# Three buffers instead of two for a unit's sum of values in attention (gated mix of attention and a routed expert layer, one core)

## The chip, the cores and the metric

The kernel runs on one core of one Trainium2 chip. The metric is the time of one execution on the device in microseconds (us). The kernel before takes 1399.78 us, the median of three runs from 1396.5 to 1401.64.

## The reference, cut to what matters

The input x has 2048 rows of 448 numbers. Two branches read it, and a gate per row mixes them.

```python
def _A_ref(x, wqkv, wo):                 # 16 heads of 28
    q, k, v = ...                        # x @ wqkv, by heads
    scores = jnp.einsum("bhqd,bhkd->bhqk", q, k) * scale
    p = _softmax(scores, axis=-1)
    o = jnp.einsum("bhqk,bhkd->bhqd", p, v)
    return o.transpose(0, 2, 1, 3).reshape(B, S, D) @ wo

def _B_ref(x, w_gate, w1, w2):           # 8 experts, the best 2 of each row
    ...
    for e in range(E):
        out = out + w * (_silu(xf @ w1[e]) @ w2[e])

g = _sigmoid((x * gate_w).sum(-1, keepdims=True))
return g * a + (1 - g) * b
```

The change lies in `p @ v`, the sum of the values weighted by the softmax.

## The kernel before, in words

The work has four stages, one after the other on one core: the projections of x to q, k, v and the routing; the experts (with the maxima of the scores computed beside them); attention; and the projection with wo, which also adds the experts' part and writes the output.

**Attention.** The 16 heads are taken in four groups g of four heads, and the 2048 queries in four stretches qc of 512. A *unit* u = 4 g + qc is one group and one stretch, so there are 16 units. A unit has eight steps p, each with two tiles of 128 keys, so there are 128 steps m = 8 u + p. The loop at L1228 emits for each m: `scores(m + 1)`, `beside(m)`, `values(m)`.

- `scores(m)` (L1161) computes the scores of two key tiles for four heads (TensorE, L733) into PSUM, and takes their exponentials on ACT (L1173, L1174, L1176, L1177) into the tile P. One of the eight banks is first copied to SBUF by DVE (X, L1175). At p = 0 it also loads the next unit's queries (`load_q`, L719 and L721, on SP).
- `values(m)` (L1180) multiplies P with the values V (TensorE, L1188) into a bank of PSUM, `po`. DVE then moves that bank into the unit's sum in SBUF, the tile `osb`: a copy at p = 0 (L1192), an addition at the other steps (L1194).
- `beside(m)` (L1196) emits the rest between the two. For the unit before, u - 1, it brings the softmax's denominators, which are a row of `osb`, through DRAM and back: `collect_sums` at p = 0 (POOL issues, L1110 and L1112), `invert_sums` at p = 3 (L1116), `spread_sums` at p = 4 (L1122). At p = 7 `divide(u - 1)` multiplies `osb` by the reciprocals on DVE (L1127), in place, and SP issues four to six transfers (L1137) from it to its rows of the tile OT, which the last stage reads. It also gathers the experts' rows with POOL (`fetch_routed` at p = 1, L1064, tile yg), adds them on DVE at p = 2, 4, 5 and 6 (`routed`, from L1073), and loads the next group's keys and values on SP (`load_k` L704 and L707 at p = 3 and 6, `load_v` L691 at p = 4, and at p = 0 of the next group's first unit).

**The order of the work.** PE, DVE, ACT and POOL execute in the order in which the code emits (`manual_schedule`, L1141); the order of what SP issues is left to the scheduler. A tile name has as many buffers as `bufs` says, by default that of its pool: two in the pool `pc_sb` (L1042), from which `osb`, X and P come. The next use of a buffer waits for the last reader of its former tile. The banks of PSUM that the scores of one key tile and the values share, z0 and z1 (`single`, L1150), have one buffer each and alternate from step to step.

So the tile `osb` of unit u stands in the same buffer as that of unit u - 2. Unit u - 2 is divided, and its transfers to OT are issued, at the last step of unit u - 1. The copy L1192 of unit u comes one step later.

Of the kernel before, what the change touches and what calls it, by code (L numbers as in the profile page):

```python
# [8 lines left out]
F32 = mybir.dt.float32  # L9
# [53 lines left out]
def tile_gated_mha_moe(ctx: ExitStack, tc: tile.TileContext, x, xe_, xT, wv, wqk, wo, w1, w2, out):  # L63
# [213 lines left out]
    with ExitStack() as pa:  # L277
        sb = pa.enter_context(tc.tile_pool(name="pa_sb", bufs=1))
# [459 lines left out]
    with ExitStack() as pb:  # L738
        sb1 = pb.enter_context(tc.tile_pool(name="pb_sb1", bufs=2, reuse_waits="tile"))
        sb = pb.enter_context(tc.tile_pool(name="pb_sb", bufs=2, reuse_waits="tile"))  # L740
# [301 lines left out]
    sb = ctx.enter_context(tc.tile_pool(name="pc_sb", bufs=2, reuse_waits="tile"))  # L1042
# [102 lines left out]
    accs, rc, rs = {}, {}, {}  # L1145
# [4 lines left out]
    def single(i):  # L1150
        return ps.tile([128, 512], F32, name=f"z{i % 2}")
# [28 lines left out]
    def values(m):  # L1180
        u, p = divmod(m, NPR)
        P = Pc.pop(m)
        po = single(m + 1)
        for i in range(2):
            kt = 2 * p + i
            v = held[u // 4][1][kt // 8]
            for j in range(4):
                nc.tensor.matmul(po[32 * j:32 * j + 32], v[:, kt % 8, 32 * j:32 * j + 32], P[4 * i + j],  # L1188
                                 start=i == 0, stop=i == 1)
        if p == 0:  # L1190
            accs[u] = sb.tile([128, 512], F32, name="osb")
            nc.vector.tensor_copy(accs[u], po)  # L1192
        else:
            nc.vector.tensor_tensor(accs[u], po, accs[u], op=ALU.add)  # L1194
# [33 lines left out]
    for m in range(NU * NPR):  # L1228
        if m + 1 < NU * NPR:
            scores(m + 1)  # L1230
        beside(m)
        values(m)
# [70 lines left out]
```

## Time and profile before

| | us |
|---|---|
| median of three runs | 1399.78 |
| the profiled execution | 1399.52 |
| its span, first to last instruction | 1397.7 |
| before attention's steps | 0 to 836 |
| attention's steps | 836 to 1358 |
| the last projection | 1358 to 1397.7 |

The mean granted clock of TensorE over the span is 0.988. The profile is read as follows. PE is TensorE's matrix products, PEld its weight loads, DVE the vector engine, ACT the scalar engine, POOL GpSimd, SP the engine that issues most transfers (SPq: its queue). A row of the order of time gives the start, the duration, the engine, the line, the operation, the tiles written and read, and in brackets how long the engine stood idle before it and what ended that. A row of waits gives who waited for whom, the sum, the times and the longest. A row of stretches gives the bounds, the length, the busy time of PE, PEld, DVE, ACT and POOL with the number of instructions, the granted clock of TensorE (1.00 is full speed), the busy share of the transfer engines and GB/s.

### The profile page before, as it was taken

What the parts mean: (1) busy time and instruction counts of PE and PEld (TensorE: products, weight loads), DVE (VectorE), ACT (ScalarE), POOL (GpSimd) and SP (SyncE); (2) the same over time, 40 slices, a digit from 0 to 9 for tenths busy, and PEclk for the clock granted to TensorE, in tenths of its full rate; (3) what the DMA queues carried; (4) which work ended last, traced back from release to release, by engine and by line L of the source; (5) the groups of instructions that cost most, each with busy time, mean ns of one, the idle gap of its engine ahead of it and who ended that gap; (6) DMA issues with size and microseconds to landing.
All of it is one profiled execution on the core that took longest, in us unless ns stands there. A gap on an engine that the chain in (4) does not pass through costs nothing. (4 is left out here: it accounts for less than half of the span.)

```text
span 1397.7 us, 27189 instructions
## 1 busy us (share of the span) xinstructions
PE 1353.4 (97%) x10166; PEld 892.3 (64%) x10166; DVE 927.0 (66%) x1076; ACT 849.0 (61%) x1270; POOL 616.1 (44%) x661
## 2 busy tenths in 40 slices
PE   9999999999999999999999999997999799979999
PEld 8888788788877777777777774433343333433348
DVE  5737898888988988889887854443444344434445
ACT  5335355345433543434444349997999799969871
POOL 2124676577566876668767531221222222212220
PEclk9999999999999999999999999999999999989999
DMA  9887865653444544445453221233223322422113
GB/s 348 298 282 232 299 181 174 214 176 113 146 139 149 142 150 146 151 155 168 134 165 105 73 81 56 69 86 109 68 66 97 98 57 68 125 68 61 47 50 127
DMA packets 136278, 191.30 MB, mean 137 GB/s; under 512 B 23284, under 2 KB 102680, under 8 KB 135632
## 3 DMA queue, kind: packets, MB, share of 16 engines
q1 hardware_dynamic: 124992, 160.55, 36.3%
q0 software_dynamic: 11008, 28.76, 6.8%
q8 instruction: 80, 1.31, 0.4%
q14 instruction: 54, 0.44, 0.1%
q10 hardware_dynamic: 144, 0.23, 0.1%
HBM read 139.20 MB, written 60.74 MB: 143 GB/s over the span
## 5 line engine op out<-in xcount | busy, mean ns | idle before, releaser
L143 DVE TENSOR_REDUCE mp<-pm 128x3 f32<-128x1536 f32 (+1 forms) x301 | 508.7, 1732 | 11.0 <-PE pm L122 11.0
L1188 PE MATMUL z<-P,V 128*32 128x512 f32 x2032 | 252.4, 615 | 0.2
L733 PE MATMUL z<-Q,Kh 29*128 29x512 f32 x508 | 188.0, 449 | 37.3 <-DVE osb L1192 37.3
L1176 ACT ACTIVATE P<-s 128x1536 f32<-128x1536 f32 x127 | 194.3, 1530 | 27.0 <-PE s L733 26.9
L1174 ACT ACTIVATE P<-s 128x1536 f32<-128x1536 f32 x127 | 193.8, 1526 | 0.0
L733 PE MATMUL s<-Q,Kh 29*128 29x512 f32 x1524 | 191.0, 446 | 0.0
L1175 DVE COPY X<-z 128x512 f32<-128x512 f32 x127 | 87.8, 691 | 153.8 <-PE z L733 142.2
L804 POOL TENSOR_TENSOR w2l<-w2r,w2h 128x448 fp32r<-128x448 f32 x112 | 129.3, 1155 | 118.8 <-ACT w2h L798 92.1
L1020 ACT ACTIVATE yo<-acc 128x448 f32<-128x448 f32 x64 | 34.8, 544 | 232.9 <-PE acc L1006 223.9
L733 PEld LDWEIGHTS z<-Q,Kh 29*128 29x128 f32 x508 | 75.5, 185 | 152.3 <-DVE osb L1192 41.7
L1006 PE MATMUL acc<-w2h,hh 128*128 128x448 f32 x448 | 167.6, 374 | 0.3 <-PEq L818 0.3
L1006 PE MATMUL acc<-w2h,hl 128*128 128x448 f32 x448 | 166.5, 372 | 0.0
L1006 PE MATMUL acc<-w2l,hh 128*128 128x448 f32 x448 | 166.1, 371 | 0.0
L949 ACT ACTIVATE hf<-acc 128x512 f32<-128x512 f32 (+6 forms) x154 | 74.2, 482 | 138.0 <-PE acc L945 130.4
L136 DVE TENSOR_REDUCE mp<-acc 128x1 f32<-128x512 f32 x130 | 89.4, 688 | 85.1 <-PE pm L122 83.6
L813 POOL TENSOR_TENSOR hl<-hf,hh 128x512 fp32r<-128x512 f32 x112 | 144.8, 1293 | 1.0 <-ACT hh L952 1.0
L1188 PEld LDWEIGHTS z<-P,V 128*32 128x32 f32 x2032 | 54.1, 111 | 133.1 <-issue 85.1
L1194 DVE TENSOR_TENSOR osb<-z,osb 128x512 f32<-128x512 f32 x112 | 77.4, 691 | 91.3 <-PE z L1188 91.3
L945 PE MATMUL acc<-xeh,w1h 128*128 128x512 f32 (+3 forms) x408 | 136.8, 339 | 0.0
L945 PE MATMUL acc<-xeh,w1l 128*128 128x512 f32 (+3 forms) x408 | 136.1, 338 | 0.0
L1110 POOL DMA_DIRECT2D sum_d<-osb x64 | 31.0, 491 | 204.5 <-DVE osb L1194 204.3
L772 POOL TENSOR_TENSOR w1l<-w1r,w1h 128x1024 fp32r<-128x1024 f32 (+1 forms) x49 | 90.9, 1854 | 61.5 <-ACT w1h L766 48.0
(221 smaller groups left out, 2777.2 us busy)
## 6 DMA issues: line engine op xcount, KB each, us to landing
w2r<-in_w_dram SPq DMA_DIRECT2D x112, 224.0 KB
w1r<-in_w_dram SPq DMA_DIRECT2D x56, 384.0 KB
ys_d<-zero_d SPq DMA_DIRECT2D x32, 448.0 KB
ys_d<-yo SPq DMA_DIRECT2D x64, 224.0 KB
x_d<-xf SPq DMA_DIRECT2D x115, 64.0 KB
qkh_d<-hi SPq DMA_DIRECT2D x28, 256.0 KB
qkl_d<-lo SPq DMA_DIRECT2D x28, 256.0 KB
w1r<-in_w_dram SPq DMA_DIRECT2D x112, 64.0 KB
```

Of the source, the lines that this page charges most:

```text
L136: nc.vector.tensor_reduce(mp[:, o:o + 1], banks[0], axis=AX.X, op=ALU.max)
L143: nc.vector.tensor_reduce(mp[:, (o + lo) % 256:(o + lo) % 256 + hi - lo], pm[h][:, lo - 3 * h:hi - 3 * h], axis=AX.X, op=ALU.max)
L733: nc.tensor.matmul(banks[j], k[rw, ks], q[rw, c], start=i == 0, stop=i == 2)
L772: nc.gpsimd.tensor_tensor(l[:, :, half], r[:, :, half], h[:, :, half].bitcast(F32), op=ALU.subtract)
L804: nc.gpsimd.tensor_tensor(w2l, w2r, w2h.bitcast(F32), op=ALU.subtract)
L813: nc.gpsimd.tensor_tensor(hl, hf32, hh[:, 0:512].bitcast(F32), op=ALU.subtract)
L945: nc.tensor.matmul(pu[:, 0:HC], a, b[:, cs], start=i == 0, stop=i == len(mms) - 1)
L1006: nc.tensor.matmul(py[:n, 0:D], a[:, cs], b, start=i == 0, stop=i == 3 * NH - 1)
L1174: nc.scalar.activation(P[:, 1:4], t[0], AF.Exp, scale=SCALE)
L1175: nc.vector.tensor_copy(X, z[1])
L1176: nc.scalar.activation(P[:, 4:7], t[1], AF.Exp, scale=SCALE)
L1188: nc.tensor.matmul(po[32 * j:32 * j + 32], v[:, kt % 8, 32 * j:32 * j + 32], P[4 * i + j], start=i == 0, stop=i == 1)
```

## The change

The tile `osb` gets three buffers instead of the pool's two. Nothing else differs.

```diff
         if p == 0:
-            accs[u] = sb.tile([128, 512], F32, name="osb")
+            accs[u] = sb.tile([128, 512], F32, name="osb", bufs=3)
             nc.vector.tensor_copy(accs[u], po)
         else:
             nc.vector.tensor_tensor(accs[u], po, accs[u], op=ALU.add)
```

The tile of unit u then stands in the buffer of unit u - 3. One buffer takes 2 KB in each of the 128 partitions of SBUF.

## The prediction

> **What bounds the kernel now.** I read the page first, for which engine looks full.
>
> ```profile
> span 1397.7 us, 27189 instructions
> ## 1 busy us (share of the span) xinstructions
> PE 1353.4 (97%) x10166; PEld 892.3 (64%) x10166; DVE 927.0 (66%) x1076; ACT 849.0 (61%) x1270; POOL 616.1 (44%) x661
> ```
>
> PE's 97% leaves 44 us, but the share is an average over stages. The change touches only attention's second part (L1161 to L1194), which runs from 836 to 1358 us, so the next view is busy time by stretch: all of attention, then unit 1 alone (eight steps without a stall), units 2 to 14, and two short stretches.
>
> ```profile
> 836.00:1358.00 522.00, 484.49 (x5085) 196.67 (x5078) 226.52 (x366) 471.32 (x509) 108.21 (x182) 0.97 0.27 76
> 865.90:895.38 29.48, 29.48 (x327) 11.97 (x320) 13.83 (x22) 29.48 (x34) 7.19 (x13) 1.00 0.21 61
> 895.38:1326.50 431.12, 396.57 (x4168) 161.67 (x4160) 184.69 (x297) 385.71 (x418) 92.01 (x157) 0.96 0.28 79
> 1063.48:1066.90 3.42, 3.42 (x24) 1.39 (x20) 0.73 (x2) 1.04 (x2) 0.96 (x1) 0.50 0.78 228
> 1333.14:1336.55 3.41, 3.41 (x21) 1.01 (x21) 1.97 (x4) 1.97 (x2) 0.00 (x0) 0.50 0.63 233
> ```
>
> The columns after the length are busy time of PE, PEld, DVE, ACT and POOL, then the granted clock. In unit 1 ACT is busy for all of 29.48 us: the exponentials of one step follow each other without a gap, 29.48 / 8 = 3.685 us a step. PE fills that time too, at full clock. In units 2 to 14 ACT is idle for 431.12 - 385.71 = 45.4 us and the mean clock is 0.96. So the stage has a floor, ACT's 3.685 us a step, and something lifts it off that floor once a unit. The waits name it:
>
> ```profile
> engine line waited for: us in total, times, longest us
> ACT P L1176 <- PE s L733: 26.9, 7, 8.0
> ACT P L1173 <- PE s L733: 23.3, 15, 3.0
> ...
> PE z L733 <- DVE osb L1192: 37.3, 14, 8.5
> ...
> DVE osb L1192 <- DMA OT<-osb: 55.0, 14, 10.1
> ```
>
> ACT waits for PE's scores, PE waits for DVE's copy L1192 to free a bank of z, and the copy waits, in 14 of 16 units, for a transfer. The order of time at the start of unit 7 shows why:
>
> ```profile
> 1054.21 0.68 DVE L1127 TENSOR_TENSOR osb<-osb,rs 128x512 f32<-128x512 f32 x1
> 1054.92 4.11 SPq L1137 DMA_DIRECT2D OT<-osb  x5
> 1061.02 0.69 DVE L1192 COPY osb<-z 128x512 f32<-128x512 f32 x1 [2.09 <-DMA OT<-osb]
> 1061.77 0.49 PE L733 MATMUL z<-Q,Kh 29*128 29x512 f32 x1 [1.42 <-DVE osb L1192]
> ```
>
> The sum of unit 5 is divided in the last step of unit 6, then SP issues five transfers out of it (4.11 us). Unit 7's first copy wants the same buffer one step later, and on DVE it blocks what is queued behind it: the next step's X copy and the additions.
>
> **The change part by part.** With three buffers unit u's first copy writes the buffer of unit u-3, whose transfers went out a whole unit (29 us) earlier. The wait of 55.0 us goes; no instruction, transfer or wait is added, nothing is moved. The price of the wait is not PE's 37.3 us but what the units last beyond 29.48 us. For units 2 to 14: 431.12 - 13 x 29.48 = 47.9 us. For unit 15 the ACT rows give the stalled stretch, two steps long:
>
> ```profile
> 1326.50 1.56 ACT L1174 ACTIVATE P<-s 128x1536 f32<-128x1536 f32 x1
> ...
> 1338.80 1.45 ACT L1174 ACTIVATE P<-s 128x1536 f32<-128x1536 f32 x1
> ```
>
> 12.30 - 2 x 3.685 = 4.9 us. Together 52.8 us: 37.3 of them PE standing still, the rest mostly PE running at half clock after the longer stalls. The two stretches at clock 0.50 above lie behind the stalls of units 7 and 15, whose waits of PE are (in the windows 1050 to 1065 and 1325 to 1340 us):
>
> ```profile
> PE z L733 <- DVE osb L1192: 1.4, 1, 1.4
> ...
> PE z L733 <- DVE osb L1192: 2.9, 1, 2.9
> ```
>
> In unit 1, with no such wait, the clock is 1.00, so I let the half-clock stretches go with the stalls.
>
> [...]
>
> What is late next? First yg: step p=2 of a unit starts adding what POOL gathered shortly before.
>
> ```profile
> 873.66 0.69 DVE L1175 COPY X<-z 128x512 f32<-128x512 f32 x1 [1.12 <-PE z L733]
> 874.27 0.61 DVE L1073 TENSOR_TENSOR yg<-yg 128x448 f32<-128x448 f32 x1
> 875.54 0.69 DVE L1194 TENSOR_TENSOR osb<-z,osb 128x512 f32<-128x512 f32 x1 [0.65 <-PE z L1188]
> ...
> 899.50 1.03 POOL L1064 DMA_INDIRECT yg<-ys_d,slot_i  x1 [0.30 <-issue]
> ...
> 930.73 1.03 POOL L1064 DMA_INDIRECT yg<-ys_d,slot_i  x1 [0.30 <-issue]
> ...
> DMA to landing us min/median/max: 4.0/4.2/5.2
> ...
> 925.45 1.56 ACT L1174 ACTIVATE P<-s 128x1536 f32<-128x1536 f32 x1
> ```
>
> L1073 is due 874.27 - 865.90 = 8.37 us into a stall-free unit, and DVE has 0.65 us to spare before the addition that PE waits for. Unit 2 (from 895.38): due at 903.75, landed at 899.50 + 4.2 = 903.70, on time. Unit 3 (from 925.45): due at 933.82, landed at 934.93; 1.11 - 0.65 = 0.46 us late. Until now the stall hid this. Bounds over 14 units: 0 if all are like unit 2; (930.73 + 5.2 - 933.82 - 0.65) x 14 = 1.46 x 14 = 20.4 us if all issue as late as unit 3 and land at the slowest. I take half the units like unit 2 and half like unit 3: 7 x 0.46 = 3.2, and about half of it, 1.5 us, since the X copy and PE's queue have a little slack of their own.
>
> Second, V's other half at units 4, 8 and 12, issued behind the OT transfers and first needed at p=4.
>
> ```profile
> 1220.57 1.56 ACT L1174 ACTIVATE P<-s 128x1536 f32<-128x1536 f32 x1
> ...
> 880.91 1.92 PE L1188 MATMUL z<-P,V 128*32 128x512 f32 x16
> ...
> 1227.16 0.48 SPq L691 DMA_DIRECT2D V<-v_d  x1
> ...
> 1231.00:1233.60 2.60, 1.11 (x9) 0.83 (x9) 0.69 (x1) 0.00 (x0) 0.00 (x0) 0.50 0.56 164
> 1233.60:1235.60 2.00, 2.00 (x13) 0.40 (x12) 0.69 (x1) 1.83 (x2) 0.00 (x0) 0.50 0.00 0
> ```
>
> In unit 1 p=4 begins 880.91 - 865.90 = 15.0 us in, so in unit 12 without the stall at 1235.6. The DMA share (last column but one) falls to 0.00 after 1233.6: V is there with 2.0 us to spare. I cost it at 0, and 0 to 3 us a boundary as bounds.
>
> Third, memory: a third 2 KB a partition shifts tiles behind osb in the pool, and so which old tile each waits for when attention opens.
>
> ```profile
> 836.04 0.60 ACT L1173 ACTIVATE P<-z 128x512 f32<-128x512 f32 x1 [0.39 <-PE s L733]
> ...
> 838.46 0.96 POOL L1064 DMA_INDIRECT yg<-ys_d,slot_i  x1 [21.50 <-DMA wo_r<-in_wo_dram]
> ```
>
> The last transfers of the stage before have landed when the first gather starts, so a shifted tile costs at most 838.46 - 836.04 = 2.4 us, once. It could also end one of the waits there, so the other bound is the 0.39 us before that first exponential, as a gain. I take 0, since P and X are asked for ahead of osb.
>
> The sum: the profiled execution took 1399.5 us (1.8 us outside its span; the runs' median is 1399.8). 1399.5 - 52.8 + 1.5 = 1348.2. The projections after 1358 us only start earlier.
>
> **The rivals.**
>
> One, the gather becomes the new bound in every unit: for it, unit 3's lateness; against, unit 2's. 1346.7 + 20.4 = 1367. Chance 0.06.
>
> Two, the group boundaries: SP's order is not written out by hand, and the scheduler may plan it anew when a wait goes; V or K then lands after its need. At 2 us of slack, a 5 us slip costs 3 us and, as in unit 7, a half-clock stretch of 3.42 x 0.5 = 1.7 us: 3 x 4.7 = 14, so 1362. For it, DMA is dense there (share 0.56); against, V's issue does not wait for the stalled copy. Chance 0.07.
>
> Three, the half-clock stretches after short waits come from elsewhere and stay: 2 x 1.7 = 3.4 us, 1351.6. Against it, the clock of unit 1. Chance 0.04. [...]
>
> Four, slower than before: PE, no longer resting once a unit, loses clock throughout. PE fills its step of 3.685 us at clock 1.00; over the 112 steps of units 2 to 15 the 52.8 us are used up when a step takes 3.685 + 0.47 = 4.16 us, at a clock below 0.89. At 0.85 a step takes 4.34 us and the time is 1348.2 + 112 x 0.65 = 1421. Against it, 29.48 us without a pause were granted 1.00. Chance 0.02.
>
> Five, the buffer does nothing, because the copy's wait is kept for a reason other than the buffer (the transfers' tile OT, say): 1399.5. Against it, the copy touches only z and osb. Chance 0.03.
>
> **How the numbers follow.** The main case has 0.78, at 1348.2. Its range is 1343.5 (no late gather, and 3 us of spread as the runs show, 1396.5 to 1401.6 around 1399.8) to about 1356 (one unit's slip or a shifted tile on top). Reaching to rival two gives 1343 to 1362; left out are rivals one, four and five and the odd tail. A measurement of this kernel can tell about 0.5%, 7 us, from no change. Faster by more takes the main case and rivals one to three: 0.95. Within 0.5% is rival five and a little more: 0.03. Slower: 0.02.
>
> **What would show it.** Right: no wait of L1192 for OT; in the ACT rows every unit from 1 to 15 lasts 29.5 to 30.2 us; the clock in attention is 1.00; L1073 gets a short wait for yg; attention ends near 1307 us. Wrong: units 4, 8 and 12 still last several us longer (rival two), or all do (rival one), with PE waiting for an L1194 that stands behind L1073; PE at a clock below 1 without an idle stretch ahead of it.

## The result, and the profile after

The changed kernel takes 1353.13 us (median of four runs, 1352.16 to 1354.23); beside it the kernel before took 1400.51 us. The ratio is 0.967, 95% interval 0.965 to 0.969. The profiled execution took 1352.68 us, with a span of 1350.9 us: 46.8 us less than before, where the forecast had 51.3.

The same views as before the change. Busy time by stretch: attention, unit 1, units 2 to 13, unit 14, and one short stretch in unit 14.

```profile
836.00:1310.00 474.00, 471.25 (x5079) 191.41 (x5074) 227.16 (x365) 468.93 (x509) 108.58 (x182) 1.00 0.30 84
865.78:895.27 29.49, 29.49 (x328) 11.92 (x320) 13.88 (x22) 29.49 (x34) 7.19 (x13) 1.00 0.21 61
895.27:1250.96 355.69, 354.81 (x3848) 144.64 (x3840) 170.24 (x272) 354.35 (x385) 84.91 (x145) 1.00 0.33 92
1250.96:1284.27 33.31, 31.46 (x328) 12.44 (x320) 15.11 (x25) 29.71 (x34) 7.08 (x13) 0.95 0.18 50
1260.93:1264.35 3.42, 3.42 (x16) 0.53 (x16) 1.22 (x2) 1.79 (x2) 0.00 (x0) 0.50 0.00 0
```

Attention is 48 us shorter, and ACT's busy time in it is about the same (468.93 us against 471.32): the same work without the gaps. Units 2 to 13 are 355.69 - 12 x 29.48 = 1.9 us above the floor. Unit 14 alone is 3.8 us above it, and has the only stretch of attention at half clock.

The waits of DVE in attention:

```profile
DVE osb L1194 <- PE z L1188: 80.9, 103, 2.3
DVE osb L1192 <- PE z L1188: 11.5, 13, 1.3
...
DVE yg L1073 <- DMA yg<-ys_d,slot_i: 6.5, 7, 2.0
DVE oh L1086 <- DMA OT<-osb: 2.1, 1, 2.1
DVE osb L1192 <- DMA OT<-osb: 1.2, 1, 1.2
```

The copy L1192 no longer waits 55.0 us for OT. What it waits now is the 1.2 us for the product that unit 1 had before as well; the last row is one more wait of that length, and its releaser was only the last to report. Two waits stand where none stood: L1073 for the gathered yg, and L1086 for OT. The second, in the order of time (DVE and SP, in unit 14):

```profile
1249.48 6.14 SPq L1137 DMA_DIRECT2D OT<-osb  x8
...
1255.06 0.69 DVE L1175 COPY X<-z 128x512 f32<-128x512 f32 x1 [1.13 <-PE z L733]
1257.86 0.43 DVE L1086 CAST oh<-OT 128x512 fp32r<-128x512 f32 x1 [2.12 <-DMA OT<-osb]
1258.32 0.56 DVE L180 TENSOR_TENSOR ol<-OT,oh 128x384 fp32r<-128x384 f32 x1
1258.89 0.29 DVE L181 TENSOR_TENSOR oh<-OT,oh 64x128 fp32r<-64x128 f32 x1
1259.21 0.69 DVE L1194 TENSOR_TENSOR osb<-z,osb 128x512 f32<-128x512 f32 x1
```

Unit 12 is divided at the last step of unit 13. It has eight transfers, as each unit of the last group has, and not the four to six that the description gives; they take SP 6.14 us to issue, and the first split of OT for the last projection (`split_o`, at p = 1 of unit 14) needs them. DVE waits 2.12 us, then does 1.3 us of splitting (each value into a rounded part and a rest), and only then the addition that frees PE's bank.

### The profile page after: what moved, and what is told of

The parts are those of the page before. It is cut to its first block, busy times and chain, and to the rows that moved or that the text cites. A ratio compares the mean times of both kernels' runs of the same rounds, so it can differ in the third digit from the quotient of the medians.

```text
span 1350.9 us, 27181 instructions
## 1 busy us (share of the span) xinstructions
PE 1341.4 (99%) x10166; PEld 887.2 (66%) x10166; DVE 928.1 (69%) x1076; ACT 847.5 (63%) x1270; POOL 616.6 (46%) x661
## 5 line engine op out<-in xcount | busy, mean ns | idle before, releaser
L1188 PE MATMUL z<-P,V 128*32 128x512 f32 x2032 | 246.4, 602 | 0.0
L1176 ACT ACTIVATE P<-s 128x1536 f32<-128x1536 f32 x127 | 198.1, 1560 | 0.9 <-PE s L733 0.9
L1174 ACT ACTIVATE P<-s 128x1536 f32<-128x1536 f32 x127 | 196.5, 1547 | 0.0
L733 PEld LDWEIGHTS z<-Q,Kh 29*128 29x128 f32 x508 | 74.5, 183 | 111.9 <-issue 30.2
L1194 DVE TENSOR_TENSOR osb<-z,osb 128x512 f32<-128x512 f32 x112 | 77.4, 691 | 82.1 <-PE z L1188 81.9
```

Source lines behind the costliest of these rows:

```text
L733: nc.tensor.matmul(banks[j], k[rw, ks], q[rw, c], start=i == 0, stop=i == 2)
L1174: nc.scalar.activation(P[:, 1:4], t[0], AF.Exp, scale=SCALE)
L1176: nc.scalar.activation(P[:, 4:7], t[1], AF.Exp, scale=SCALE)
```

## The experiments

The theory: the gain is the wait of L1192 for transfers that SP issues only one step earlier; what is missing against the forecast is L1086 in unit 14 and L1073 in units 3, 4, 5, 12 and 15, both hidden by the old stall (for units 5 and 15 this did not hold, see e5_gather). The rivals: the gain comes with the shifted memory; a third buffer is needed because the transfers as such are too slow; the remaining waits would cost anyway. Lengths of units are from the starts of L1174 on ACT, every eighth; the floor is 29.48 us. All ratios are to the kernel before on the same chip (1403 to 1404 us in these series). The lengths of units 0 to 14 in the profiles that matter most:

```
before         29.37 29.47 30.07 30.74 39.12 30.75 30.82 32.77 38.82 30.61 30.94 30.55 40.61 30.45 34.87
after          29.36 29.49 29.49 29.63 30.65 29.78 29.48 29.48 29.49 29.49 29.48 29.49 29.76 29.47 33.31
e2_div6        29.38 29.56 30.29 29.50 30.34 29.67 29.72 29.59 30.71 29.51 29.59 29.51 30.40 29.51 29.65
e8_three_div6  29.37 29.49 29.49 29.57 29.49 29.75 29.70 29.57 29.51 29.56 29.48 29.56 29.48 29.49 29.84
```

**The layout alone (e1_pad).** Two buffers, and a tile of 2 KB behind them in which one element is written.

```diff
             accs[u] = sb.tile([128, 512], F32, name="osb")
+            if u == 0:
+                pad = sb.tile([128, 512], F32, name="pad", bufs=1)
+                nc.gpsimd.memset(pad[0:1, 0:1], 0.0)
```

> Two buffers for osb as before, and one more tile of 2 KB a partition asked for right behind it, of which one element is written once and none is read: the memory layout of the changed kernel without its third buffer. If the gain is the wait of L1192 for the transfers out of osb: the wait stays at about 55 us, the time at 1400 (1396 to 1403). If the gain came from the shifted layout: about 1353.

Measured: ratio 0.9997 (0.998 to 1.001). DVE's wait (the copy is L1195 here) is what it was:

```profile
DVE osb L1195 <- DMA OT<-osb: 55.1, 14, 9.1
```

The layout has no part in the gain.

**The same wait removed in another way (e2_div6).** Two buffers; the division one step earlier.

```diff
-        if u and p == 7:
+        if u and p == 6:
             divide(u - 1)
```

> Two buffers as before, but the division of unit u-1 one step earlier (p=6 instead of 7), so that its transfers are issued ahead of the next queries and one step sooner. Theory (the copy waits for transfers that are issued only one step before it): most units reach about 29.6 us without a third buffer; at units 4, 8 and 12 the transfers now stand behind the second half of K instead of behind K and the queries, so 2 to 4 us stay at each; about 0.15 us a unit is lost because division and the last routed addition share p=6 on DVE. 1358 (1352 to 1366), at least three quarters of the gain. Rival (a buffer more is needed because the sums and the transfers as such are too slow): under a third of the gain, above 1385.

Measured: 1355.08 us, ratio 0.9655 (0.964 to 0.967): not told apart from the third buffer's 0.967, without its 2 KB. The order of time at the boundary of unit 12, in the kernel before (SP, then DVE):

```profile
1216.85 1.62 SPq L704 DMA_DIRECT2D Kl<-qkl_d  x4
1218.51 1.67 SPq L719 DMA_DIRECT2D Q<-qkh_d  x4
1220.22 1.68 SPq L719 DMA_DIRECT2D Q<-qkl_d  x4
1221.95 1.13 SPq L721 DMA_DIRECT2D Q<-m_d  x4
1223.18 3.88 SPq L1137 DMA_DIRECT2D OT<-osb  x5
...
1217.89 0.68 DVE L1127 TENSOR_TENSOR osb<-osb,rs 128x512 f32<-128x512 f32 x1
1231.74 0.69 DVE L1192 COPY osb<-z 128x512 f32<-128x512 f32 x1 [10.09 <-DMA OT<-osb]
```

And with the early division:

```profile
1192.20 1.61 SPq L704 DMA_DIRECT2D Kl<-qkl_d  x4
1193.91 3.85 SPq L1137 DMA_DIRECT2D OT<-osb  x5
1197.80 1.83 SPq L719 DMA_DIRECT2D Q<-qkh_d  x4
...
1199.25 0.69 DVE L1192 COPY osb<-z 128x512 f32<-128x512 f32 x1 [2.15 <-PE s L733]
```

At this boundary the transfers now stand ahead of the queries, and the copy starts 1.0 us later than unhindered (2.15 us of idle time, where 1.17 are usual) instead of 9 us (PE, named in that row, was only the last to report). Units 4, 8 and 12 are 0.9, 1.2 and 0.9 us above the floor, not 2 to 4 us as expected: I had the landing too slow (transfers out of osb landed 1.6 to 2.0 us after their issue here). The rival that needs a third buffer falls. Unit 14 is at 29.65 us, since unit 12's transfers leave early too.

**The queue on SP (e11_query_later).** Two buffers, division at p = 7; the next queries are asked for one step later, behind the transfers.

```diff
-        if p == 0 and u and u + 1 < NU:
+        if p == 1 and u and u + 1 < NU:
             qs[u + 1] = load_q((u + 1) // 4, (u + 1) % 4)
```

> Two buffers and the division at p=7, as before; only the twelve loads of the next queries are asked for one step later, so that SP issues the transfers out of osb ahead of them. Theory (the long stalls of units 4, 8 and 12 are the queue on SP: K and the queries, 4.5 us of issuing, stand ahead of transfers that have one step of time): these units and 7, 14 and 15 fall by 3 to 7 us each, to 31 to 35 us, the short stalls of the others stay at 0.6 to 1.5 us; 1375 (1365 to 1385). Rival (the landing of the transfers is slow whatever their place in the queue): above 1392.

Measured: 1375.79 us, ratio 0.979 (0.978 to 0.981). The time is as expected, its make-up not quite: the scheduler put the transfers ahead of the queries only at the three group boundaries, and elsewhere left all but one of the twelve loads in front. SP and DVE at the boundary of unit 12, and DVE's wait in all:

```profile
1203.32 1.61 SPq L704 DMA_DIRECT2D Kl<-qkl_d  x4
1205.50 3.85 SPq L1137 DMA_DIRECT2D OT<-osb  x5
1209.39 1.83 SPq L719 DMA_DIRECT2D Q<-qkh_d  x4
...
1210.84 0.69 DVE L1192 COPY osb<-z 128x512 f32<-128x512 f32 x1 [2.29 <-DMA OT<-osb]
...
DVE osb L1192 <- DMA OT<-osb: 32.0, 14, 4.6
```

Units 4, 8 and 12 fell from 39.12, 38.82 and 40.61 us to 30.53, 30.41 and 30.43 us, 27.2 us together, which is about the whole gain here (28.1 us) and half of the 52.8 us; unit 14, which waits for the eight transfers of unit 12, stayed at 34.38 us. Units 14 and 15 were expected to fall by 3 us or more and hardly moved (the two stalled steps of unit 15 last 12.35 us), unit 7 fell by 2.1 us, and units 3 and 10 rose to 32.89 and 32.38 us. So about half of the old stall was the place of the transfers at three boundaries, behind 4.5 us of queries; K costs little there, since SP had issued it by 1218.47 us in the kernel before, where the division ended at 1218.57. For the other half the place and the short time are not told apart: elsewhere eleven of the twelve loads still stood in front, and e2_div6 changed both, the time and the place (there ten of the twelve loads came behind the transfers, at the boundaries all).

**A fourth buffer (e3_four).** `bufs=4` in place of 3.

> Four buffers instead of three. Theory: the copy L1192 waits for no transfer with three, so a fourth changes nothing: 1353 (1350 to 1356). Rival (part of the 4.5 us that the forecast had too much are waits for a buffer still): 1349 or less.

Measured: ratio 0.967 (0.965 to 0.969), as with three. The time in us (1357.47) belongs to a series in which the kernel before took 1403.79; the ratio is what compares. A fourth buffer of osb gives nothing that shows.

**The two later limits with two buffers (e7_two_both).** The first split moved to p = 3 and the gathers moved ahead (the edits of e4_split and e5_gather below), in the kernel before.

> Two buffers as before, with both later limits of the changed kernel taken away: the gathers of yg three to four steps earlier, and the first split of OT at p=3 of unit 14 instead of p=1. Theory (the stall of L1192 hides both limits, and they only cost once it is gone): 1400, within 3 us of before. Rival (they cost on their own, before too): 1393 to 1395.

Measured: ratio 0.9993 (0.998 to 1.001), as the theory has it. The equal time alone does not show that both limits were hidden, since the edits move units both ways: unit 0 is 3.6 us longer (32.96 us, see e5_gather), and units 2 to 14 are 3.2 us shorter in all. The profile before shows it: neither L1073 nor L1086 waits for a transfer there.

**The first split of OT later (e4_split).** Three buffers.

```diff
-    WHOLE_O = [(NU - 2, 1), (NU - 1, 0), (NU - 1, 1)]
+    WHOLE_O = [(NU - 2, 3), (NU - 1, 0), (NU - 1, 1)]
```

> Three buffers, and the first split of OT (L1086) two steps later, at p=3 of unit 14 instead of p=1. Theory (unit 14's 33.31 us are DVE's wait for the transfers of unit 12, divided five steps before, and the half clock that follows): unit 14 falls to 29.5 to 29.8 us, the time by 3.5 to 3.8 us to 1349 to 1350; the half-clock stretch in attention goes. Rival (these transfers are late whatever asks for them, or p=3, which holds the inversion of the sums, is too full on DVE): unit 14 stays above 31 us, 1351 to 1353.

Measured: 1352.22 us, ratio 0.9636 (0.962 to 0.965); 0.0031 less than with three buffers alone is 4.3 us (each ratio is good to about 0.002). Unit 14 lasts 29.58 us, the wait of L1086 is gone, and the longest wait of PE that is left is 0.6 us, where three buffers alone leave one of 1.85 us. The theory holds, except that the transfers of unit 12 follow a division two steps before L1086, not five.

**The gathers earlier (e5_gather).** Three buffers.

```diff
-        if p == 1:
-            fetch_routed(u)
+        if (u, p) == (0, 1):
+            fetch_routed(0)
+        if p == 5 and u + 1 < NU:
+            fetch_routed(u + 1)
```

> Three buffers, and the gathers of yg for unit u+1 issued at p=5 of unit u instead of p=1 of unit u+1. Theory (units 3, 4, 5, 12 and 15 lose 2 us in all to L1073 waiting for yg): the 6.5 us of such waits go, these units fall to 29.5 us, the time by about 2 us to 1351. Rival (the gathers, 0.9 MB a unit, now delay the reciprocals or the second half of K): DVE or PE waits for those instead, 1353 or more.

Measured: ratio 0.9669 (0.965 to 0.968), no gain. The waits of L1073 are gone, and units 3, 4 and 12 are at 29.57, 29.41 and 29.41 us. Unit 5 is not shorter (29.91 us against 29.78), so its excess is not shown to be yg. In unit 15 L1073 never waited: the late addition there stands right behind the split of OT (in the changed kernel L181 ends at 1290.61 us, and L1194 starts at 1290.64). Against the gain, unit 0 rose from 29.36 to 32.98 us, and unit 14, where L1086 waits 2.7 us here and not 2.1, from 33.31 to 35.09 us; the mean clock of the span is 0.995, against 0.998 with three buffers alone. In unit 0 POOL now issues four gathers in a row, and beside them DVE starts late (DVE, order of time):

```profile
842.08 0.69 DVE L1192 COPY osb<-z 128x512 f32<-128x512 f32 x1 [1.27 <-PE z L1188]
844.87 0.69 DVE L1175 COPY X<-z 128x512 f32<-128x512 f32 x1 [2.10 <-PE z L733]
847.76 0.69 DVE L1194 TENSOR_TENSOR osb<-z,osb 128x512 f32<-128x512 f32 x1 [2.20 <-PE s L733]
```

Why DVE is late there is open: the scores that the X copy reads were done at 843.8 us. e7_two_both has the same unit 0 (32.96 us).

**Both (e6_both).** Three buffers with the edits of e4_split and e5_gather.

> Three buffers, with the later split and the earlier gathers together. Theory (nothing else holds attention above ACT's 3.685 us a step): every unit from 1 to 15 lasts 29.4 to 29.6 us, attention's clock is 1.00, the time falls by 5.5 to 6 us against three buffers alone, to about 1347. Rival (another wait comes up behind these two): 1349 to 1352.

Measured: 1352.41 us, ratio 0.9634 (0.962 to 0.965). Units 1 to 14 are between 29.41 and 29.73 us, so attention reaches the floor; unit 0, at 31.09 us, gives part of it back. Against three buffers alone the gain is 0.0033, or 4.6 us, not the 5.5 to 6 expected.

**Three buffers and the early division (e8_three_div6).**

> Three buffers with the division at p=6. Theory (unit 14's stall is the wait for the transfers of unit 12): these leave a step earlier and the stall goes, 3.8 us; p=6 holds the last routed addition and the division on DVE, which costs 0 to 0.2 us a unit, 0 to 3 us in all: 1350 (1348 to 1353). Rival (a full p=6 delays the addition that PE waits for by the whole 0.68 us): 14 x 0.5 = 7 us more, above 1355.

Measured: 1350.13 us, ratio 0.9623 (0.961 to 0.964). Busy time over attention:

```profile
838.50:1310.00 471.50, 470.72 (x5083) 192.76 (x5080) 228.44 (x368) 469.11 (x509) 108.55 (x183) 1.00 0.31 84
```

All units lie between 29.37 and 29.84 us. The full p = 6 on DVE costs next to nothing.

**With the gathers earlier from unit 2 on (e10_two_best, e9_three_best), and the changed kernel on the same chip (e12_after_again).** The first has two buffers, the second three; both have the division at p = 6 and

```diff
-        if p == 1:
+        if p == 1 and u < 2:
             fetch_routed(u)
+        if p == 5 and 0 < u < NU - 1:
+            fetch_routed(u + 1)
```

> Two buffers, the division at p=6, and from unit 2 on the gathers of yg at p=5 of the unit before. Theory (with the division a step earlier the second buffer is enough but for short waits at units 4, 8 and 12; the rest of what is left are waits for yg): 4.8 us above the floor in the kernel with the division alone, 2 to 3 us here: 2 us less than with the division alone, a ratio to before of 0.963 to 0.965. Rival (a third buffer is needed at the group boundaries): no change against the division alone.

> Three buffers, the division at p=6, and from unit 2 on the gathers of yg at p=5 of the unit before (unit 1's stay where they were). Theory (attention is at ACT's floor but for 1.3 us with the division alone): at most 1.3 us less than that kernel, which no timing can tell; the ratio to before 0.961 to 0.963; unit 0 keeps its 29.4 us, which it lost where unit 1's gathers were issued in it. Rival (earlier gathers cost elsewhere): 0.964 or more.

> The changed kernel once more, on the chip of the three others. Ratio to before 0.966 to 0.968; unit 14 at 33 to 35 us, units 4 and 12 up to 1.5 us above 29.5, all others within 0.7 us.

Measured: 0.9650 (0.963 to 0.967), 0.9617 (0.960 to 0.963) and 0.9665 (0.965 to 0.968). The version with two buffers is not told apart from the early division alone (0.9655), so its question stays open; in its profile units 4, 8 and 12 are 0.4, 1.2 and 0.4 us above the floor. The version with three is not told apart from e8_three_div6, but is clear of the changed kernel on the same chip by 0.0048, or 6.7 us; unit 0 is back at 29.39 us. The changed kernel repeated its ratio and unit 14's 33.52 us.

## Why the prediction was right, point by point

**The bound.** Attention runs at ACT's pace, 3.685 us a step, unless something stops it: right. The kernels all but without waits reach it: in e8_three_div6 ACT is busy for 469.11 of 471.50 us, and in e9_three_best no wait of ACT shows from 840 to 1311 us.

**The price of the wait.** 52.8 us from what the units last beyond the floor, not PE's 37.3 us. Units 2 to 14 stood 47.9 us above the floor before and stand 5.8 us above it now; the two steps of unit 15's old stall went from 12.30 to 7.41 us. That is 42.1 + 4.9 = 47.0 us of the span's 46.8. The rest, 5.8 us, is what came up behind. That the half clock belongs to the stalls was right: its stretches behind the 1.4 and 2.9 us waits are gone. Six such stretches stood in attention before; these four and the two shown in the prediction hold 23.9 us of busy PE; if half of it is lost, an estimate from their granted clock of 0.50, then 37.3 + 12 = 49 us of the 52.8 are accounted for.

```profile
1227.32:1237.56 10.24, 5.07 (x25) 1.42 (x25) 1.38 (x2) 1.97 (x2) 0.00 (x0) 0.50 0.44 143
1299.00:1302.42 3.42, 3.42 (x25) 0.77 (x17) 1.87 (x4) 1.97 (x2) 0.00 (x0) 0.50 0.48 152
...
964.50:971.32 6.82, 4.34 (x25) 1.43 (x25) 1.38 (x2) 1.97 (x2) 0.00 (x0) 0.50 0.50 155
1097.62:1104.44 6.82, 4.23 (x25) 1.43 (x25) 1.38 (x2) 1.97 (x2) 0.00 (x0) 0.50 0.54 166
```

**The gathers.** Forecast 1.5 us, measured about 1.6 us (units 3, 4 and 12: 0.14, 1.16 and 0.28; e5_gather takes nearly all of it away). Named rightly, but that the size fits is luck: the forecast spread the loss over half the units at 0.46 us each and then halved it. Unit 3, its model, lost 0.14 us, units 6 to 8 waited for yg without being longer, and most of the loss was in unit 4, at a group boundary.

**V and the layout.** Both costed at 0. No wait of PE for V shows in the changed kernel, and e1_pad shows the layout at 0.

**What failed.** The list of what is late next stopped at yg, V and the layout; L1086 was not on it, though in unit 14 it is due at 1255.75 us, 0.1 us after SP has issued the last of unit 12's transfers (1249.48 + 6.14 = 1255.62). Unit 14's 3.8 us are nearly all of the 4.5 us by which the forecast was too low, as e4_split shows. "Attention ends near 1307 us" (it was 1310) and a clock of 1.00 throughout failed by that unit; "every unit from 1 to 15 lasts 29.5 to 30.2 us" failed by it and by unit 4 (30.65 us). The text had looked at the transfers to OT only as what L1192 waited for, not at who else reads OT.

**The rivals.** None of them came. The gather did not bind in every unit, SP's order stayed as it was, row for row, the half clock left with PE's long waits (units 2 to 13, with one wait of 0.88 us left, had a clock of 1.00), and PE at full load, busy for 470.72 of 471.50 us in e8_three_div6, kept the clock of 1.00.

## What to carry to other kernels

A wait for a buffer has two cures: one buffer more, or an earlier end of the old use; here one step earlier was as good as 2 KB, and both together were better than either (0.962 against 0.9655 and 0.967; against the first of these the intervals just touch). Price a stall by what its stage lasts beyond its floor, and before counting the gain list every reader of every tile that the waiting transfers write: who else had been covered by the stall is the next to wait.

## What the runs showed of the hardware

TensorE's clock was at half beside long waits of PE and beside some short ones. In attention of the kernel before, PE waited 14 times for DVE. The waits of 7.34, 1.42, 7.08, 8.46, 3.49 and 2.94 us, in units 4, 7, 8, 12, 14 and 15, were each overlapped or followed by one of the six stretches at 0.50, 3.41 to 10.24 us long. The other eight waits, of 0.30 to 1.16 us, were not: between the six stretches the clock was 1.00. In the changed kernel the wait of 1.85 us in unit 14 was followed by 3.42 us at 0.50, and the one of 0.88 us in unit 4 by none. In e11_query_later the clock was 0.51 from 934.97 to 938.38 us, and the one wait of PE between 920 and 940 us was of 1.5 us.
